# A fused attention and two-FFN kernel: whole token tiles through DRAM in FFN2, and another order of the seven block products of a pair

## The chip, the cores and the metric

The kernel runs on one core of a Trainium2 chip. The metric is the device time of one execution in microseconds, the median over the runs. A profile of one further execution comes with it; its span runs from the first to the last instruction of the program.

## The reference, cut to what matters

Sliding-window attention over 4 batches of 576 tokens with 8 heads gives x of 2304 tokens by 512. Two feed-forward layers follow; the change lies in the second.

```python
x = attention(q, k, v)                        # 2304 x 512, window of 64
h = np.maximum(x @ w_in, 0.0)                 # FFN1, 2048 wide
x = h * h @ w_out                             # 2304 x 512
h = x @ w2_in                                 # FFN2, 1024 wide
e = np.exp(h - np.max(h, axis=-1, keepdims=True))
solu = h * (e / (np.sum(e, axis=-1, keepdims=True) + 1e-09))
mu, var = np.mean(solu, -1, keepdims=True), np.var(solu, -1, keepdims=True)
out = ((solu - mu) / np.sqrt(var + 1e-06) * g_ln) @ w2_out
```

## The kernel before

Everything is fp32, computed on TensorE as three fp32r products per block: each operand is split into a high part (ScalarE copies it, which rounds) and a low part (VectorE subtracts the high part), and high*high, high*low and low*high are accumulated (`TERMS`).

**The planner.** No order is written out by hand. The kernel's Python first adds some 2,400 tasks with `add(engine, us, rank, fn, after, take, give, ...)`: a duration, a rank, the tasks that it waits for, and the buffers that it takes and gives back (`wb`, `wm`, `raw`, `g`, `a`, `b`, `t`, ...; `a`, `b` and `t` are PSUM tiles of the pools `ps_a`, `ps_b` and `ps_t`). `Plan.run` plays them through: of all tasks whose waits are met it takes the one that can start first, and the lower rank where two could start at once. Each engine gets its instructions in that order and runs them in order. `SHIFT` adds a number to the rank of single tasks, by their number. 51 filler matmuls (`warm`, line 1766, rank 900) stand wherever the planner sees nothing else for TensorE.

**The stages.** Attention and FFN1 are interleaved up to about 385 us. The sweep (line 1070, `swept`) finishes FFN1's last pass: it loads intermediates `r` from DRAM, splits them (`parted`, lines 1091 and 1094, tiles `g` and `gx`) and multiplies. The first weights of FFN2 are made meanwhile (`w2_operands`). FFN2 begins at 438.6 us and lasts to the end.

**FFN2.** `pair2` takes two token tiles of 128 at a time, nine pairs in all. The 256 x 1024 product of a pair with `w2_in` is made with seven block products in place of eight (a Strassen form): x is cut into A11, A12, A21, A22 (tile by half of the 512 inputs), the sums S1 to S4 are made from them on VectorE, and the weights have T1 to T4. A product is two times three matmuls of 512 columns (line 1543). The products add up in four PSUM banks named a, b, c, d:

```
P1 = A11 B11 (a)   P2 = A12 B21 (b)   P3 = S4 B22 (c)   P4 = A22 T4 (d)
P5 = S1 T1 (c)     P6 = S2 T2 (a)     P7 = S3 T3 (a)
C11 = P1 + P2      C12 = (P1 + P6) + (P5 + P3)
C21 = (P1 + P6 + P7) + P4             C22 = (P1 + P6 + P7) + P5
```

Where a bank is added to after it was needed as it stood, ScalarE copies it first (`keep1`, line 1549, tile `p`; `u2`, line 1553; `u3`, line 1557), and `total` (line 1568) makes each C block on VectorE from a bank and a copy or another term, with the running minimum that the softmax needs.

**Behind the products.** `behind` takes one tile of 128 tokens by 1024: exp on ScalarE (line 1625), the SoLU product on VectorE (1632), centring on ScalarE (1636), then a transpose. It is made of two VectorE transposes of 32 x 32 blocks (`blocks2`, line 1652, one per half of the 1024), a store to DRAM (`aside`, line 1656) and four loads with the blocks in their places (`across`, line 1664). ScalarE and VectorE split the loaded tile (`t_high`, line 1684; `t_low`, line 1688, tile `lnT`), and `mm_o` (line 1695) multiplies by `w2_out`, 12 matmuls for each half. All DMAs of this part are issued from SyncE's queue.

Of the kernel before, what the change touches and what calls it, by code (L numbers as in the profile page):

```python
# [20 lines left out]
P = 128  # L21
# [5 lines left out]
class Plan:  # L27
# [10 lines left out]
    SHIFT = {0: 19.99, 1: 13.18, 37: 14.79, 71: -15.08, 162: -7.47, 183: 14.39, 188: 6.06, 192: -2.38, 195: 10.82, 198: 10.82, 228: 5.72, 260: -3.03,  # L38
# [69 lines left out]
def kernel(  # L108
# [96 lines left out]
    with ExitStack() as c1:  # L205
# [1206 lines left out]
        def w2_operands(r, rank, homes):  # L1412
# [27 lines left out]
            for x in ("B11", "T2", "T3", "T1", "B21", "T4", "B22"):  # L1440
                if x in ("T1", "T4"):
                    when[x][1].append(ready["T2" if x == "T1" else "T3", r])
                ready[x, r] = split(hi[x], lo[x], *when[x], rank, 512, src[x], ["raw"] * (x in ("T1", "T4")))
                w2i[x, r] = hi[x], lo[x]
# [36 lines left out]
        ring = {}  # L1481
        kept = []
# [4 lines left out]
        def pair2(n, rank, rank_o):  # L1487
# [41 lines left out]
            def product(bank, x, w, begins, ends):  # L1529
                if begins and n < 2 and bank in "ad" and bank not in o:  # L1530
                    o[bank] = ps_a.tile([P, 512], F32, tag="a", name="ps_h2")
                elif begins and bank not in o:
                    if n in (0, 2):
                        kept.append(ps_b.tile([P, 2, 512], F32, tag="b", name="ps_h2"))
                    o.update(c=kept[0][:, 0], b=kept[0][:, 1])
                    if n > 1:
                        o.update(a=kept[1][:, 0], d=kept[1][:, 1])
# [59 lines left out]
            free = read_of.get(n - 1, {})  # L1597
            p1 = pe(0, "a", "A11", "B11", True, free.get("a", []) if n > 1 else [], take=["a"] if n < 2 else ["b"] * (n == 2))
# [15 lines left out]
            for m, k in enumerate((1, 0)):  # L1614
                behind(k, tiles[k][0], o, rank + LATE0 * (n == 0) + 0.1 * m, rank_o + m * 2 * mm(512), [f11, f12] if k == 0 else [f21, f22])
# [204 lines left out]
```

## Time and profile before

| | |
|---|---|
| median of 3 runs | 637.67 us (637.28 to 638.97) |
| the profiled execution | 637.17 us |
| its span | 635.4 us |
| mean granted TensorE clock | 0.999 |
| TensorE matmul busy | 623.2 us, 98% of the span |
| VectorE / ScalarE busy | 486.3 us (77%) / 431.0 us (68%) |

The profiled execution took 1.8 us more than its span and lies 0.5 us below the median. PE is TensorE's matmuls, PEld its weight loads, DVE is VectorE, ACT ScalarE, SP SyncE (SPq: its DMA issues). A matmul's record is longer than its turn, since the next one starts before it ends; stalls are therefore read from the distance between starts. Fillers count as busy.

### The profile page before, as it was taken

To read this page: it belongs to the slowest core of one execution; us is meant where nothing else is said; L and a number is where in the kernel's file an instruction comes from. 1 tells how busy PE (TensorE), PEld (TensorE's weight loads), DVE (VectorE), ACT (ScalarE), POOL (GpSimd) and SP (SyncE) were. 2 spreads that over 40 slices of the span, in tenths; PEclk is the share of its full clock that TensorE was granted. 3 is DMA by queue.
4 is the path that set the end of the run, shared out by engine and by line. 5 is a ranking of instruction groups with operands and counts; after the bars stand their busy time and mean duration, and the time that the engine had idled before them with its cause. 6 is when DMAs were issued, how large, how long until landed. Compare 5 with 4: busy or idle time off the path is not lost.

```text
span 635.4 us, 11735 instructions
## 1 busy us (share of the span) xinstructions
PE 623.2 (98%) x4009; PEld 523.6 (82%) x4009; DVE 486.3 (77%) x1129; ACT 431.0 (68%) x976; POOL 45.5 (7%) x80
## 2 busy tenths in 40 slices
PE   9999999999999999999999999999999999999997
PEld 4798888889889999998788887688778877778886
DVE  6999897497967653678899998998788927967450
ACT  5879776577877665657677766774677836866461
POOL 1000000001221110000000000000010200101000
PEclk9999999999999999999999999999999999999999
DMA  8888889447899999936776566864366642654451
GB/s 287 295 287 288 305 275 315 133 156 258 261 341 281 343 310 294 359 123 204 256 263 244 182 219 222 304 211 150 100 186 184 185 142 79 197 159 130 134 179 54
DMA packets 109260, 141.28 MB, mean 222 GB/s; under 512 B 9104, under 2 KB 75408, under 8 KB 109200
## 3 DMA queue, kind: packets, MB, share of 16 engines
q1 hardware_dynamic: 108512, 140.14, 66.8%
q8 instruction: 31, 0.51, 0.3%
q10 hardware_dynamic: 688, 0.39, 0.2%
q14 instruction: 29, 0.24, 0.1%
HBM read 90.69 MB, written 49.81 MB: 221 GB/s over the span
## 4 chain that ended last, share of the span: by engine, by line
PE 76%; DVE 9%; DMA 5%; ACT 3%; issue 3%; SPq 2%; POOL 0%; DVEq 0%; ACTq 0%; POOLq 0%
PE ps_h L936 18%; PE ps_h L1543 10%; PE ps_y L1256 10%; PE ps_o L1695 9%; PE ps_y L1070 8%; PE ps_y L707 7%; PE ps_h L691 6%; PE ps_s L436 2%; SPq L1664 2%; DMA tt_dram<-tt 2%; PE ps_warm L1766 2%; PE ps_v L519 2%; DVE e L1632 1%; DVE h L1568 1%; ACT e L451 1%
## 5 line engine op out<-in xcount | busy, mean ns | idle before, releaser
L1695 PE MATMUL ps_o<-w2o,lnT 128*128 128x512 f32 x432 | 100.4, 389 | 0.0
L1695 PEld LDWEIGHTS ps_o<-w2o,lnT 128*128 128x128 f32 x432 | 81.0, 188 | 17.2 <-issue 0.4
L1256 PE MATMUL ps_y<-g,wb 128*128 128x384 f32 x384 | 70.9, 335 | 0.0
L1256 PEld LDWEIGHTS ps_y<-g,wb 128*128 128x128 f32 x384 | 66.7, 188 | 0.5 <-issue 0.2
L1543 PE MATMUL ps_h<-w2i,xx 128*128 128x512 f32 x243 | 64.7, 393 | 1.8 <-DVE nmax L1568 1.0
L1070 PE MATMUL ps_y<-g,wb 128*128 128x512 f32 x234 | 58.3, 392 | 0.2 <-DVE g L1094 0.2
L1543 PEld LDWEIGHTS ps_h<-w2i,xx 128*128 128x128 f32 x243 | 45.2, 188 | 13.4 <-DVE nmax L1568 2.8
L936 PE MATMUL ps_h<-xa,wo 128*128 128x512 f32 (+1 forms) x192 | 53.0, 369 | 0.0
L1070 PEld LDWEIGHTS ps_y<-g,wb 128*128 128x128 f32 x234 | 43.6, 188 | 10.4 <-DVE g L1094 1.3
L936 PE MATMUL ps_h<-xb,wo 128*128 128x384 f32 (+1 forms) x192 | 51.2, 357 | 0.0
L707 PE MATMUL ps_y<-g,wb 128*128 128x512 f32 (+1 forms) x240 | 47.9, 352 | 0.0
L691 PE MATMUL ps_h<-x,wa 128*128 128x512 f32 (+1 forms) x240 | 47.4, 351 | 0.0
L936 PE MATMUL ps_h<-xo,wo 128*128 128x512 f32 (+1 forms) x128 | 47.2, 369 | 0.0
L451 ACT ACTIVATE e<-e,nmax 128x128 f32<-128x128 f32 x112 | 43.3, 390 | 2.2 <-DVE nmax L440 2.2
L707 PEld LDWEIGHTS ps_y<-g,wb 128*128 128x128 f32 x240 | 38.5, 189 | 6.3 <-issue 0.7
L691 PEld LDWEIGHTS ps_h<-x,wa 128*128 128x128 f32 x240 | 38.5, 189 | 6.1 <-issue 0.3
L936 PEld LDWEIGHTS ps_h<-xa,wo 128*128 128x128 f32 x192 | 35.2, 188 | 4.9 <-issue 0.3
L1543 PE MATMUL ps_h<-w2x,xx 128*128 128x512 f32 x135 | 37.2, 393 | 1.1 <-ACT p L1549 1.0
L936 PEld LDWEIGHTS ps_h<-xb,wo 128*128 128x128 f32 x192 | 34.6, 188 | 3.8 <-issue 0.5
L640 DVE TENSOR_TENSOR g<-r,g 128x384 fp32r<-128x384 f32 (+2 forms) x36 | 20.4, 569 | 21.6 <-ACT g L637 19.6
L1688 DVE TENSOR_TENSOR lnT<-l,lnT 128x512 fp32r<-128x512 f32 x36 | 24.5, 681 | 16.2 <-ACT lnT L1684 15.5
L1684 ACT ACTIVATE lnT<-l 128x512 fp32r<-128x512 f32 x36 | 22.4, 623 | 15.5 <-PE ps_o L1695 8.8
(181 smaller groups left out, 1258.6 us busy)
## 6 DMA issues: line engine op xcount, KB each, us to landing
wraw<-in_w_out SPq DMA_DIRECT2D x24, 511.8 KB, 5.0
wraw<-in_w_in SPq DMA_DIRECT2D x24, 511.8 KB, 5.5
t_dram<-h SPq DMA_DIRECT2D x36, 256.0 KB, 2.6
l<-t_dram SPq DMA_DIRECT2D x144, 64.0 KB, 2.0
vt<-in_v SPq DMA_DIRECT2D x32, 256.0 KB, 3.9
wo_dram<-wo SPq DMA_DIRECT2D x16, 512.0 KB, 4.5
wo<-wo_dram SPq DMA_DIRECT2D x16, 512.0 KB, 4.6
kt<-in_k SPq DMA_DIRECT2D x16, 384.0 KB, 5.2
```

What stands on the lines that cost most here:

```text
L436: T.matmul(to, qt[rows, i, hp, :], kt[rows, keys, hp, :], start=not begins, stop=not begins or hp == hps[-1])
L451: S.activation(out=o["er"][:, a, w], in_=s, func=AF.Exp, scale=SCALE if begins else -1.0, bias=o["nmax"][:, a, w : w + 1], accum_out=o["su ...
L640: V.tensor_tensor(out=o["g"][:, 1, :N], in0=o["r"], in1=o["g"][:, 0, :N].bitcast(F32), op=ALU.subtract)
L691: T.matmul(ps[:, :N], wa[kk][:, wi, c * P : c * P + P], xs[t][:, xi, c, n0:n1], start=n == 0, stop=n == 3 * DC - 1)
L707: T.matmul(acc[t, 0][d][:, n0:n1], wb[kk][:, wi, d * P : d * P + P], o["g"][:, xi, :N], start=kk == 0 and n == 0 and n0 == 0, stop=last an ...
L936: T.matmul(to[:, :N], w["t"][:, wi, off + c * P : off + c * P + P], (lo if xi else hi)()[:, c], start=begins and m == 0, stop=m == 5, skip ...
L1070: T.matmul(acc[name][d][:, :N], wb[kk][:, wi, col + d * P : col + d * P + P], q["g"][:, xi, :N], start=j == 0 and n == 0 and name not in ( ...
L1256: T.matmul(acc[t, half][d][:, :N], wb[kk][:, wi, d * P : d * P + P], q["g"][:, xi, :N], start=pos == 0 and n == 0, stop=pos == KF - 1 and ...
L1543: T.matmul(o[bank], o["xx", k][:, xi, at : at + P], w2i[w, r][wi][0](), start=begins and m == 0, stop=m == 5, skip_group_check=True)
L1684: S.activation(out=parts2(o["l", hf][:, 0]), in_=turned2(hf), func=AF.Copy)
L1688: V.tensor_tensor(out=parts2(l[:, 1]), in0=turned2(hf), in1=parts2(l[:, 0].bitcast(F32)), op=ALU.subtract)
L1695: T.matmul(o["o"], o["l", hf][:, xi, kk % 4, :], w2o[kk][:, wi, :], start=kk == 0 and n == 0, stop=kk == KF2 - 1 and n == 2)
```

## The change

Four things change, all but one in FFN2.

1. Token tiles go to DRAM and back whole: one store and four loads per tile, once both halves are transposed, in place of two stores and eight loads by halves. The last pair keeps its halves.
2. The products of a pair come in the order P1 P2 P5 P6 P4 P3 P7, before P1 P2 P6 P5 P7 P4 P3. P5 and P4 are copied out of their banks (`u5`, `u4`) where P1 + P6 + P7 was (`u3`); C22 and C21 are then summed from bank a and those copies. Banks a and d of odd pairs lie in `ps_t`, those of even pairs from the third on in `ps_b`; only the first pair takes them from `ps_a`. Tile 0 of a pair goes ahead of tile 1.
3. The weights of FFN2 are split in the order of the new products.
4. `SHIFT` has other numbers, for tasks of all stages; most lie in the sweep and after it.

```diff
-    SHIFT = {0: 19.99, 1: 13.18, 37: 14.79, 71: -15.08, 162: -7.47, 183: 14.39, 188: 6.06, 192: -2.38, 195: 10.82, 198: 10.82, 228: 5.72, 260: -3.03,
...
+    SHIFT = {0: 13.59, 3: 4.48, 4: -11.32, 22: -7.17, 37: 14.79, 71: -15.08, 162: -5.57, 188: 6.06, 192: -3.28, 195: 10.82, 198: 10.82, 202: -1.28,
...
+             1289: -1.64, 1297: -1.6, 1312: 1.85, 1317: 7.05, 1365: 7.1, 1457: 7.13, 1458: 6.02, 1459: 4.98, 1471: -17.49, 1493: -2.7, 1502: 16.22,
+             1504: 7.12, 1568: -7.42, 1572: -9.29, 1576: -9.35, 1580: -9.31, 1584: -9.27, 1585: 6.83, 1590: 3.97, 1592: -9.29, 1598: 10.55,
...
-            for x in ("B11", "T2", "T3", "T1", "B21", "T4", "B22"):
+            for x in ("B11", "B21", "T1", "T2", "T4", "B22", "T3"):
...
             def product(bank, x, w, begins, ends):
...
+                if begins and bank not in o:
+                    if n == 0 and bank in "ad":
+                        o[bank] = ps_a.tile([P, 512], F32, tag="a", name="ps_h2")
+                    elif n % 2 and bank in "ad":
+                        if (1, bank) not in banks:
+                            banks[1, bank] = ps_t.tile([P, 512], F32, tag="t", name="ps_h2")
+                        o[bank] = banks[1, bank]
+                    else:
+                        two = "cb" if bank in "cb" else "ad"
+                        if two not in banks:
+                            banks[two] = ps_b.tile([P, 2, 512], F32, tag="b", name="ps_h2")
+                        o[bank] = banks[two][:, two.index(bank)]
...
-            def u3():
-                o["u3"] = term("u3")
-                S.activation(out=o["u3"], in_=o["a"], func=AF.Copy)
+            def u4():
+                o["u4"] = term("u4")
+                S.activation(out=o["u4"], in_=o["d"], func=AF.Copy)
+
+            def u5():
+                o["u5"] = term("u5")
+                S.activation(out=o["u5"], in_=o["c"], func=AF.Copy)
...
-                total(1, 1, o["c"], o["u3"], True)
+                total(1, 1, o["a"], o["u5"], True)
...
-                total(1, 0, o["d"], o["u3"], False)
+                total(1, 0, o["a"], o["u4"], False)
...
-            p6 = pe(2, "a", "S2", "T2", False, [e1, p2])
+            f11 = add("DVE", 0.70, soon, c11, [p2, e1], take=["wb"])
+            p5 = pe(2, "c", "S1", "T1", True, [p2, *free.get("c", [])])
+            e5 = add("ACT", 0.60, soon, u5, [p5], take=["wm"])
+            p6 = pe(3, "a", "S2", "T2", False, [e1, p5])
             e2 = add("ACT", 0.60, soon, u2, [p6, *gone_by, *free.get("c", [])])
-            f11 = add("DVE", 0.70, soon, c11, [p2, e1], take=["wb"])
-            p5 = pe(3, "c", "S1", "T1", True, [p6, *free.get("c", [])])
-            p7 = pe(4, "a", "S3", "T3", False, [p5, e2])
-            e3 = add("ACT", 0.60, soon, u3, [p7], take=["wm"], give=["a"] * (n < 2))
-            p4 = pe(5, "d", "A22", "T4", True, [p7, *free.get("d", [])], take=["a"] * (n < 2))
-            f22 = add("DVE", 0.68, soon, c22, [p5, e3], take=["wb"])
-            f21 = add("DVE", 0.68, soon, c21, [p4, f22], give=["a", "wm"] if n < 2 else ["wm"])
-            p3 = pe(6, "c", "S4", "B22", False, [p4, f22], give=["wb"] * 4)
-            f12 = add("DVE", 0.68, soon, c12, [p3, f11, f21])
-            phase_of[n], read_of[n] = [p3], {"a": [e3], "b": [f11], "c": [f12], "d": [f21]}
+            p4 = pe(4, "d", "A22", "T4", True, [p6, *freer.get("d", [])], take=[own] if own else [])
+            e4 = add("ACT", 0.60, soon, u4, [p4], take=["wm"], give=["a"] * (n == 0))
+            p3 = pe(5, "c", "S4", "B22", False, [e5, p4])
+            f12 = add("DVE", 0.68, soon, c12, [p3, f11, e2])
+            p7 = pe(6, "a", "S3", "T3", False, [p3, e2], give=["wb"] * 4)
+            f22 = add("DVE", 0.68, soon, c22, [p7, e5], take=["wb"], give=["wm"])
+            f21 = add("DVE", 0.68, soon, c21, [p7, e4, f22], give=["wm"] + ["a"] * (n == 0))
+            phase_of[n], read_of[n] = [p7], {"a": [f22, f21], "b": [f11], "c": [f12], "d": [e4]}
...
-            for m, k in enumerate((1, 0)):
+            for m, k in enumerate((0, 1)):
...
-            by_pe = i in TURNED
+            by_pe, at_once = i in TURNED, not p["last"]
...
+            def part_c(x, hf):
+                return x if at_once else half_c(x, hf)
...
+                if at_once:
+                    p_ = [add("SP", 0.5, rank, lambda: aside(0), p_, late=2.2, give=["wb"])]
+                    p_ = [add("SP", 1.9, rank, lambda: across(0), p_, take=["g"], late=LATE_T + 0.4)] * 2
+                else:
+                    p_ = [add("SP", 0.5, rank, lambda hf=hf: aside(hf), [p_[hf]], late=1.9, give=["wb"] * hf) for hf in range(2)]
+                    p_ = [add("SP", 1.9, rank, lambda hf=hf: across(hf), [p_[hf]], take=["g"] * (1 - hf), late=LATE_T) for hf in range(2)]
```

## Rows read from the trace of the kernel before

**Rows 1.** The page's part 1: busy us, share of the span, instructions.
```profile
PE 623.2 (98%) x4009; PEld 523.6 (82%) x4009; DVE 486.3 (77%) x1129; ACT 431.0 (68%) x976; POOL 45.5 (7%) x80
```

**Rows 2.** Windows: length, busy us of each engine, clock, DMA share, GB/s.
```profile
385.00:438.60 53.60, 51.64 (x222) 40.64 (x221) 49.95 (x88) 37.26 (x69) 0.00 (x0) 1.00 0.68 224
517.00:537.00 20.00, 18.08 (x76) 14.12 (x77) 9.88 (x28) 8.88 (x15) 1.18 (x2) 1.00 0.25 75
```

**Rows 3.** PE's timeline in FFN2: start, length, matmuls; idle time and its releaser.
```profile
515.01 1.52 PE L1543 MATMUL ps_h<-w2i,xx 128*128 128x512 f32 x6
517.20 0.96 PE L1543 MATMUL ps_h<-w2x,xx 128*128 128x512 f32 x3 [0.67 <-ACT p L1549]
...
522.09 0.84 PE L1543 MATMUL ps_h<-w2i,xx 128*128 128x512 f32 x3
523.62 0.96 PE L1543 MATMUL ps_h<-w2i,xx 128*128 128x512 f32 x3 [0.69 <-ACT u L1557]
...
528.70 0.86 PE L1543 MATMUL ps_h<-w2i,xx 128*128 128x512 f32 x3
530.59 0.97 PE L1543 MATMUL ps_h<-w2i,xx 128*128 128x512 f32 x3 [1.03 <-DVE nmax L1568]
...
569.44 1.52 PE L1543 MATMUL ps_h<-w2i,xx 128*128 128x512 f32 x6
571.26 0.97 PE L1543 MATMUL ps_h<-w2x,xx 128*128 128x512 f32 x3 [0.30 <-ACT p L1549]
...
601.57 30.08 PE L1695 MATMUL ps_o<-w2o,lnT 128*128 128x512 f32 x132
```

**Rows 4.** PE's timeline ahead of the first output matmul.
```profile
456.69 1.69 PE L1766 MATMUL ps_warm<-ones 128*128 128x512 bf16 x4
458.02 1.75 PE L1543 MATMUL ps_h<-w2i,xx 128*128 128x512 f32 x6
459.61 2.33 PE L1766 MATMUL ps_warm<-ones 128*128 128x512 bf16 x10
461.88 2.97 PE L1695 MATMUL ps_o<-w2o,lnT 128*128 128x512 f32 x12
```

**Rows 5.** PE's waits from 385 to 636 us: in total, times, longest.
```profile
PE ps_y L1070 <- DVE gx L1094: 1.9, 2, 1.1
```

**Rows 6.** Groups by line, 440 to 640 us: busy, mean ns, idle before.
```profile
L1568 DVE CUSTOM_DVE_ANT_0 h<-ps_h,u,nmax 128x512 f32<-128x512 f32 x18 | 13.4, 744 | 2.0 <-PE ps_h L1543 1.0 <-DVE nmax L1568 0.5
L1557 ACT ACTIVATE u<-ps_h 128x512 f32<-128x512 f32 x9 | 5.4, 598 | 19.0 <-PE ps_h L1543 19.0
```

**Rows 7.** DMA issues: count, KB each, median us from issue to landing.
```profile
t_dram<-h SPq DMA_DIRECT2D x36, 256.0 KB, 2.6
l<-t_dram SPq DMA_DIRECT2D x144, 64.0 KB, 2.0
wo_dram<-wo SPq DMA_DIRECT2D x16, 512.0 KB, 4.5
x_dram<-y SPq DMA_DIRECT2D x1, 512.0 KB, 2.7
```

**Rows 8.** Timeline of the other engines around the first tile.
```profile
452.34 1.30 DVE L1652 STREAM_TRANSPOSE h<-e 128x512 f32<-128x512 f32 x2
453.07 1.24 SPq L1656 DMA_DIRECT2D t_dram<-h  x2
455.62 3.66 SPq L1664 DMA_DIRECT2D l<-t_dram  x8
459.38 0.61 ACT L1684 ACTIVATE lnT<-l 128x512 fp32r<-128x512 f32 x1
461.07 0.65 DVE L1688 TENSOR_TENSOR lnT<-l,lnT 128x512 fp32r<-128x512 f32 x1
462.91 0.69 DVE L1525 TENSOR_TENSOR xx<-xs,xx 128x512 fp32r<-128x512 f32 x1
```

**Rows 9.** Timeline of ACT near the end.
```profile
620.81 0.63 ACT L1684 ACTIVATE lnT<-l 128x512 fp32r<-128x512 f32 x1 [2.04 <-PE ps_o L1695]
```

More of the change, by code (lines that the diff above doesn't have):

```diff
@@ L1439, in w2_operands @@
                     "T2": ([t4], []), "T4": ([t4], [])}
-            for x in ("B11", "T2", "T3", "T1", "B21", "T4", "B22"):
-                if x in ("T1", "T4"):
-                    when[x][1].append(ready["T2" if x == "T1" else "T3", r])
-                ready[x, r] = split(hi[x], lo[x], *when[x], rank, 512, src[x], ["raw"] * (x in ("T1", "T4")))
+            for x in ("B11", "B21", "T1", "T2", "T4", "B22", "T3"):
+                if x in ("T2", "T3"):
+                    when[x][1].append(ready["T1" if x == "T2" else "T4", r])
+                ready[x, r] = split(hi[x], lo[x], *when[x], rank, 512, src[x], ["raw"] * (x in ("T2", "T3")))
                 w2i[x, r] = hi[x], lo[x]
@@ L1479, in term @@
             return raw_p.tile([P, 512], F32, tag="wm", name=name, bufs=WMB)
-        ring = {}
-        kept = []
+        ring, banks = {}, {}
         phase_of, read_of = {}, {}
@@ L1529, in product @@
             def product(bank, x, w, begins, ends):
[L1530 to L1537, printed above, removed]
+                if begins and bank not in o:
[10 more added lines that the diff above has]
+                        o[bank] = banks[two][:, two.index(bank)]
                 k, half = WHERE[x]
@@ L1596, in pair2 @@
             soon = rank - 41.25
-            free = read_of.get(n - 1, {})
-            p1 = pe(0, "a", "A11", "B11", True, free.get("a", []) if n > 1 else [], take=["a"] if n < 2 else ["b"] * (n == 2))
+            free, freer = read_of.get(n - 1, {}), read_of.get(n - 2, {}) if n > 2 else {}
+            own = {0: "a", 1: "t"}.get(n)
+            p1 = pe(0, "a", "A11", "B11", True, freer.get("a", []), take=[own] if own else ["b"] * (n == 2))
             e1 = add("ACT", 0.60, soon, keep1, [p1, *gone_by, *free.get("b", [])])
@@ L1655, in aside @@
             def aside(hf):
-                nc.sync.dma_start(out=half_c(t_dram[i].rearrange("p (b c j) -> p b c j", b=4, c=KF2), hf),
-                                  in_=half_c(o["h"].rearrange("p (b c j) -> p b c j", b=4, c=KF2), hf))
+                nc.sync.dma_start(out=part_c(t_dram[i].rearrange("p (b c j) -> p b c j", b=4, c=KF2), hf),
+                                  in_=part_c(o["h"].rearrange("p (b c j) -> p b c j", b=4, c=KF2), hf))
             def across(hf):
@@ L1663, in across @@
                 for b in range(4):
-                    nc.sync.dma_start(out=half_c(o["l4"][b * rows : b * rows + rows], hf),
-                                      in_=t_dram[i].rearrange("(a p) (b c j) -> b p a c j", a=4, b=4, c=KF2)[b][:, :, 4 * hf : 4 * hf + 4])
+                    nc.sync.dma_start(out=part_c(o["l4"][b * rows : b * rows + rows], hf),
+                                      in_=part_c(t_dram[i].rearrange("(a p) (b c j) -> b p a c j", a=4, b=4, c=KF2)[b], hf))
             def turned2(hf):
@@ L1728, in behind @@
                 r = add("ACT", 1.25, rank + 3, squares, p_)
-                p_ = [add("SP", 0.5, rank, lambda hf=hf: aside(hf), [p_[hf]], late=1.9, give=["wb"] * hf) for hf in range(2)]
-                p_ = [add("SP", 1.9, rank, lambda hf=hf: across(hf), [p_[hf]], take=["g"] * (1 - hf), late=LATE_T) for hf in range(2)]
+                if at_once:
[4 more added lines that the diff above has]
+                    p_ = [add("SP", 1.9, rank, lambda hf=hf: across(hf), [p_[hf]], take=["g"] * (1 - hf), late=LATE_T) for hf in range(2)]
                 r = add("POOL", 2.0, rank, root, [r], give=["wb"])
@@ L1739, in behind @@
                 l_free[k, hf] = [a]
-            if k == 0 and p["last"]:
+            if k == 1 and p["last"]:
                 b = add("ACT", 0.35, rank_o, lambda: scaled_half(0), [a, r], take=["r"])
```

14 rows, old and new, of the table SHIFT are left out of this document.

## The prediction

> **What bounds the kernel now.** I read the page's busy shares first: TensorE (PE) is busy in 623.2 of 635.4 us [rows 1]. So a change can win only where PE stands still, and an engine that gets faster beside it wins nothing by itself. Next came the windows by stage: the granted clock is 1.00 in both stretches shown, so time is lost to waits and not to the clock. In the sweep ahead of FFN2 (385 to 438.6 us) VectorE (DVE) is busy 49.95 of 53.6 us and PE misses 1.96; in the middle of FFN2 (517 to 537) PE misses 1.92 of 20 while DVE and ScalarE (ACT) are under half busy [rows 2]. The second stretch is short of neither engine: PE is held up by an order. The timeline of PE alone shows where.
>
> A product of six matmuls lasts 1.36 us: the run of 132 at the end starts one every (30.08 - 0.39) / 131 = 0.2266 us, 0.39 being the length of one record (the last start is 631.26) [rows 3]. With that rate the stalls can be read from start times. Six matmuls from 515.01 should end their turn at 516.37, the next starts at 517.20: 0.83 lost, waiting for `p`, the copy of P1. Three from 522.09, next at 523.62: 0.85, for `u`, a copy of the a bank. Three from 528.70, next at 530.59: 1.21, for the sum that must read bank c before P3 adds to it. Six from 569.44, next at 571.26: 0.46, for `p` again. Together 3.35 us [rows 3]. All four are one pattern: a bank is read out and added to again with a single product between.
>
> The other hole is the fill of FFN2 [rows 4]. Pair 1's last product starts at 458.02 after four filler matmuls from 456.69 (1.33 us), and ten more fillers from 459.61 stand ahead of the first output matmul (line 1695) at 461.88: 2.27 us. These fillers count as PE busy, so the busy share hides them.
>
> **The change part by part.**
>
> *Product order.* Before, P1 P2 P6 P5 P7 P4 P3: P6 adds to bank a once P1 is copied, with P2 as cover (1.36 us); P7 after the copy of P1+P6, with P5 as cover; P3 adds to c after a copy of a and a DVE sum in series (0.60 + 0.74 us, [rows 6], 1.34 and the hand-overs), with P4 as cover. After, P1 P2 P5 P6 P4 P3 P7: P6 has P2 and P5 ahead of it, P3 needs only the copy of P5 and has P6 and P4, P7 needs the copy of P1+P6 and has P4 and P3. Each cover becomes 2.72 us and no DVE sum stands in the chain any more. The longest stall above is 1.21 us and the added cover 1.36, so all four go: -3.35. The wait between pairs eases too: banks a and d alternate between two places, so the next P1 does not wait for sums of the pair before, and P5 meets bank c three products after P3 as before.
>
> Cost: one more copy per pair on ACT (P5 and P4 copied, P7 no longer), 9 x 0.60 = 5.4 us [rows 6]. ACT has 11.1 of 20 us free where the stalls are [rows 2]; PE's work hides it. If ACT has an exp or a square ahead of a copy, the copy is late by about one of those, and the doubled cover is what absorbs it. The sums on DVE stay four per pair. `c21` and `c22` now both follow the last product, so the second tile starts one sum (0.74 us) later; a tile waits much longer than that for its output matmuls, except in the fill, where the first tile counts. That one is now tile 0, ready after the sixth product as tile 1 was.
>
> *Whole tiles.* Per tile two stores and eight loads become one and four. Eight load issues take 3.66 us and two stores 1.24 [rows 8], so SyncE (SP) is spared 0.62 + 4 x 0.46 = 2.5 us a tile, for 16 of 18 tiles. What is queued behind them (loads of x, stores of the output) goes out earlier; no PE stall above ends in it, so I count nothing.
>
> It costs latency of the first half. Now its store goes out at 453.07, during the second DVE transpose (1.30 us for both); the loads start at 455.62, ACT splits at 459.38, DVE at 461.07, PE starts at 461.88 [rows 4, 8]. After, the store waits for the second transpose: +0.65. It is 512 instead of 256 KB: between +0.1 (2.7 against 2.6 us to landing) and +1.9 (4.5), the latter from stores in stages with heavier traffic; the loads, 128 instead of 64 KB, add between nothing and the same again [rows 7]. In the fill only one stream of tiles is moving, so I take the row of 2.7 for the store, another 0.1 for the loads: +0.85. At best it is 0, since ACT is done at 459.99 and DVE comes 1.08 later, being busy, which could absorb it all; at worst 0.65 + 1.9 + 1.9 = 4.45. PE has nothing else there before pair 2, whose last operand DVE starts at 462.91 and ends 0.69 later, at 463.60 [rows 8]; so unless that also moves, the fill's hole can grow by no more than 463.7 - 461.88 = 1.8. The stalls that the new order takes from pairs 0 and 1 return here as a longer wait for the same first tile: no gain. The second half arrives no later than now. Beyond the fill the loss lies behind a backlog of output matmuls; at the end ACT waits 2.04 us for PE to hand back a slot, not the other way [rows 9].
>
> The Trainium skill's page "DMA: Bandwidth & Descriptors", section "Anatomy of one DMA — SWDGE (gpsimd) path", puts a transfer at about 2.0 us plus its bytes at 436 GB/s. By that a 256 KB store takes an estimated 2.6 us, as the row has it, but a 512 KB one 3.2, and a 128 KB load 0.15 more than a 64 KB one; the fill would lose an estimated 1.4 us, and the change would win 1.95. The row of 2.7 us is a single transfer.
>
> *Rank shifts.* They change the planned order in all stages: tasks are numbered as they are added, and by that count most of the changed numbers (1568 to 1700) are loads of the sweep, moved by 9 to 12 us of rank against each other, and those just above are FFN2's first weights. PE's waits in the sweep are 1.9 us in two places, both for a split on DVE, a 93% busy engine [rows 2, 5]. Below, both could go: -1.9. Above, as many again could appear: +1.9. Nothing says which, so 0. The weights' order of splitting follows the products.
>
> **The sum.** -3.35 + 0.85 + 0 = -2.5 us. The profiled execution took 637.17 us, 1.8 beyond its span, and 0.5 less than the median of 637.67; 637.17 - 2.5 = 634.67, and 637.67 - 2.5 = 635.17 as a median; I say 635.1.
>
> **The rivals.**
>
> *More than forecast.* Fill and sweep close as well: pair 2's operands are prepared earlier, since ACT and DVE are not full there, and replace fillers (up to 1.33 + 2.27 = 3.6), or the two waits of the sweep go (1.9). Against it: the first tile's chain is no shorter. With 1.9 more and half of the fill: 637.67 - 3.35 - 1.9 - 1.8 + 0.85 = 631.5.
>
> *The stall only moves.* PE has many small waits for ACT and DVE, both in-order engines. If the new order on them puts a copy behind an exp and a square, or uses up the ready output matmuls in a burst, the two stalls for `p` stay (0.83 + 0.46) and the fill takes its 1.8: -3.35 + 1.29 + 1.8 = -0.26, or 637.4. For it: DVE is near full at the seam of sweep and FFN2. Against it: DVE and ACT are under half busy where the stalls are.
>
> *Slower: the sweep starves.* The new shifts start loads of the sweep earlier, and they take shared buffers and queue turns from the splits that feed PE. Two waits cost 1.9 now, 0.95 each [rows 5]. It decides the sign once it adds more than the 2.5 won, three further waits, and measurably at five: +4.75 - 2.5 = 2.2, or 639.9. For it: DVE's 93% in that stretch leaves no slack. Against it: those loads are moved to earlier, and late loads are what starve a split.
>
> **How the numbers follow.** Forecast (stalls gone, fill a little longer) 0.42: 633.7 to 636.2. More than forecast 0.22: 630.5 to 633.7. Stall only moves 0.21: 636.2 to 638.8. Slower 0.15: 638.8 to 642. A measurement of this kernel tells 0.3% (1.9 us) from no change: faster means under 635.8, slower over 639.6. Of the forecast's 0.42 about 0.35 lies under 635.8; with 0.22 faster is 0.57. Of the slower rival's 0.15 about 0.12 lies beyond 639.6, and the rest, 0.31, is the same. The predicted time is 635.1; from 631.0 to 638.8 leaves out some 0.04 below and 0.15 above. The forecast's own range is 633.7 to 636.2.
>
> **What would show it.** In the profile after, PE should have no wait for `p`, `u` or a sum between the products of a pair; products of one pair should stand in runs with 0.227 us between starts. The hole ahead of the first output matmul, now 1.33 + 2.27 us of fillers [rows 4], should lie in one piece behind pair 1 and be longer by 0.85, at most 1.8. Stores to `t_dram` should number 20 (16 + 4) instead of 36, loads from it 80 instead of 144, and land in 2.7 and 2.1 us. If the store takes over 4 us, or output matmuls come in a long burst and PE then waits, the fill or the backlog was mis-sized; if PE's waits in the sweep pass 4 us, the shifts were.

## The result and the profile after

| | before | after |
|---|---|---|
| median | 638.32 us (637.28 to 639.49) | 631.17 us (630.62 to 631.53) |
| runs | 4 | 4 |
| ratio, with its 95% interval | | 0.9887 [0.9865, 0.9908] |
| the profiled execution | 637.17 us | 631.49 us |
| its span | 635.4 us | 629.7 us |

The change wins 7.15 us between the medians and 637.17 - 631.49 = 5.68 us between the two profiled executions; the forecast was 2.5. Before scatters more than after: over 19 runs beside the later experiments its median was 637.86 (636.25 to 641.27). What follows is worked out between the profiles, and the 1.5 us between 5.68 and 7.15 is that scatter: the profiled run of before lies 1.15 under its median of 638.32, that of after 0.32 over its own.

The first two parts of the page after, busy time and the windows, answer to [rows 1, 2].

```profile
PE 621.6 (99%) x4009; PEld 523.7 (83%) x4009; DVE 484.6 (77%) x1129; ACT 434.8 (69%) x985; POOL 45.3 (7%) x80
```

```profile
385.00:438.60 53.60, 52.16 (x225) 41.07 (x224) 51.53 (x91) 37.47 (x69) 0.00 (x0) 1.00 0.68 225
517.00:537.00 20.00, 20.00 (x90) 16.57 (x89) 14.39 (x35) 13.69 (x23) 1.75 (x4) 1.00 0.47 159
```

PE does the same 4009 matmuls, all 51 fillers among them, and is busy 1.6 us less. The fillers have moved: 8 stand inside FFN2, where 14 stood, and four behind its last output matmul. From 517 to 537 it has no gap at all, where it missed 1.92 of 20 us; the granted clock is 1.00 in both stretches, as before. PE's list of waits from 380 us on has four lines, as before, but they add up to 2.1 us in place of 4.6:

```profile
PE ps_y L1070 <- DVE y L1157: 1.0, 1, 1.0
PE ps_h L1546 <- ACT u L1560: 0.7, 1, 0.7
PE ps_h L1546 <- ACT u L1556: 0.2, 1, 0.2
PE ps_y L1070 <- DVE gx L1094: 0.2, 1, 0.2
```

PE's timeline shows what stands where the fill of FFN2 was [rows 4] (L1546 is a product, L1707 an output matmul, L1782 a filler, L1070 the sweep):

```profile
446.16 1.52 PE L1070 MATMUL ps_y<-gx,wb 128*128 128x512 f32 x6
447.52 2.12 PE L1782 MATMUL ps_warm<-ones 128*128 128x512 bf16 x7
449.29 1.04 PE L1546 MATMUL ps_h<-w2i,xx 128*128 128x512 f32 x3
...
459.04 0.39 PE L1782 MATMUL ps_warm<-ones 128*128 128x512 bf16 x1
459.08 1.04 PE L1546 MATMUL ps_h<-w2i,xx 128*128 128x512 f32 x3
...
468.33 0.96 PE L1546 MATMUL ps_h<-w2x,xx 128*128 128x512 f32 x3 [0.70 <-ACT u L1560]
...
469.82 11.04 PE L1707 MATMUL ps_o<-w2o,lnT 128*128 128x512 f32 x48
...
489.22 0.98 PE L1546 MATMUL ps_h<-w2x,xx 128*128 128x512 f32 x3 [0.19 <-ACT u L1556]
...
490.73 11.07 PE L1707 MATMUL ps_o<-w2o,lnT 128*128 128x512 f32 x48
```

Pair 0 starts before the sweep's last twelve matmuls, pair 1 follows at 449.29, and then the whole of pair 2, from 459.08 on, stands where ten fillers were. The first output matmul starts at 469.82 instead of 461.88: the first tile is 8 us later, and PE has work all the same. From there whole pairs (42 products' matmuls) and two whole tiles (48 output matmuls) take turns. The other engines' timeline says why pair 2 is ready:

```profile
458.12 0.70 DVE L1664 STREAM_TRANSPOSE h<-e 128x512 f32<-128x512 f32 x1
458.74 0.65 DVE L1524 TENSOR_TENSOR xx<-xs,xx 128x512 fp32r<-128x512 f32 x1
458.85 0.32 SPq L1668 DMA_DIRECT2D t_dram<-h  x1
...
461.97 1.83 SPq L1676 DMA_DIRECT2D l<-t_dram  x4
...
468.17 1.15 ACT L1696 ACTIVATE lnT<-l 128x512 fp32r<-128x512 f32 x2
```

DVE ends pair 2's last operand (line 1524) at 459.39, where before it ended at 463.60 [rows 8], and the first tile's transposes (line 1664), its store and its loads stand between and behind these splits. On the page the tile's transfers are half as many, twice as large, and land in 2.9 us each [rows 7]:

```profile
t_dram<-h SPq DMA_DIRECT2D x16, 512.0 KB, 2.9
l<-t_dram SPq DMA_DIRECT2D x64, 128.0 KB, 2.9
```

**Where the 5.7 us came from**, by starts in the two traces. FFN2's length below runs from its first product to the end of its last output matmul, less 12 x 0.2267 = 2.72 us where twelve matmuls of the sweep lie inside; "sweep's end" is the start of the first product plus these 2.72.

| | before | after | |
|---|---|---|---|
| sweep's end | 438.61 | 435.28 + 2.72 = 438.00 | -0.6 |
| fillers inside FFN2 | 14 in 3.60 us | 8 in 1.81 us | -1.8 |
| PE's gaps inside FFN2, those of 0.07 us and more beyond a 0.2267 us turn | 5.39 | 2.11 | -3.3 |
| FFN2's length | 193.05 | 187.92 | -5.1 |

### The profile page after: what moved, and what is told of

It reads as the page before. It is cut to its first block, busy times and chain, and to the rows that moved or that the text cites. A ratio compares the mean times of both kernels' runs of the same rounds, so it can differ in the third digit from the quotient of the medians.

```text
span 629.7 us, 11572 instructions
## 1 busy us (share of the span) xinstructions
PE 621.6 (99%) x4009; PEld 523.7 (83%) x4009; DVE 484.6 (77%) x1129; ACT 434.8 (69%) x985; POOL 45.3 (7%) x80
## 4 chain that ended last, share of the span: by engine, by line
PE 86%; DVE 5%; DMA 4%; ACT 3%; issue 1%; SPq 1%; POOL 0%; ACTq 0%; DVEq 0%; POOLq 0%
PE ps_h L936 22%; PE ps_o L1707 14%; PE ps_y L1070 10%; PE ps_h L1546 10%; PE ps_y L1256 10%; PE ps_y L707 7%; PE ps_h L691 6%; PE ps_s L436 3%; PE ps_v L519 2%; PE ps_warm L1782 1%; DMA l<-t_dram 1%; DMA kt<-in_k 1%; DMA r_dram<-u 1%; DMA t_dram<-h 1%; PE ps_v L522 1%
## 5 line engine op out<-in xcount | busy, mean ns | idle before, releaser
L1707 PE MATMUL ps_o<-w2o,lnT 128*128 128x512 f32 x432 | 99.1, 389 | 0.0
L1707 PEld LDWEIGHTS ps_o<-w2o,lnT 128*128 128x128 f32 x432 | 81.1, 188 | 16.9
L1546 PE MATMUL ps_h<-w2i,xx 128*128 128x512 f32 x243 | 62.8, 391 | 0.0
L1070 PE MATMUL ps_y<-g,wb 128*128 128x512 f32 x234 | 58.3, 391 | 1.1 <-DVE y L1157 1.0
L1546 PEld LDWEIGHTS ps_h<-w2i,xx 128*128 128x128 f32 x243 | 45.6, 188 | 9.6
L1070 PEld LDWEIGHTS ps_y<-g,wb 128*128 128x128 f32 x234 | 43.7, 188 | 11.4 <-DVE y L1157 1.4
L1546 PE MATMUL ps_h<-w2x,xx 128*128 128x512 f32 x135 | 37.0, 393 | 0.9 <-ACT u L1560 0.7
L461 POOL TENSOR_TENSOR e<-e,sums 128x512 f32<-128x512 f32 x16 | 18.5, 1179 | 205.0 <-PE ps_h L936 141.9
```

Source lines behind the costliest of these rows:

```text
L461: eng.tensor_tensor(out=o["er"][:, a], in0=o["er"][:, a], in1=o["sums"][:, a].unsqueeze(2).to_broadcast([P, HP, W]), op=ALU.mult)
L1070: T.matmul(acc[name][d][:, :N], wb[kk][:, wi, col + d * P : col + d * P + P], q["g"][:, xi, :N], start=j == 0 and n == 0 and name not in ( ...
L1546: T.matmul(o[bank], o["xx", k][:, xi, at : at + P], w2i[w, r][wi][0](), start=begins and m == 0, stop=m == 5, skip_group_check=True)
L1707: T.matmul(o["o"], o["l", hf][:, xi, kk % 4, :], w2o[kk][:, wi, :], start=kk == 0 and n == 0, stop=kk == KF2 - 1 and n == 2)
```

## The experiments

Two theories stood at the start. **The products:** the covers of 2.72 us take the stalls away, as forecast, and the shifts in FFN2 close the fill. **The queues:** the rank shifts put instructions into an order on the in-order engines in which no product's copy stands behind a wait for a load, and pair 2 ahead of the first tile; the product order itself matters little. (A third, that the spared DMA issues closed the fill, fell with e1.) Parts were undone in the kernel after or put alone into the kernel before; the new early shifts, those ahead of FFN2, were not run without the new weights' order. Tasks kept their shift's number where a part adds or drops tasks. Lengths are read as in the table above, each from one profile; profiled runs lie up to 1.3 us from the median of their kernel (e2, e10, e13), so some tenths decide nothing.

| kernel | median (range), us | ratio to before | sweep's end | FFN2 | fillers |
|---|---|---|---|---|---|
| after, tiles in halves (e1) | 630.52 (630.22 to 631.55) | 0.9884 [0.9842, 0.9926] | 437.40 | 187.58 | 8 |
| after, no FFN2 shifts (e2) | 635.61 (634.36 to 638.26) | 0.9961 [0.9943, 0.9980] | 437.10 | 191.75 | 12 |
| after, old products (e3) | 631.52 (631.12 to 632.14) | 0.9897 [0.9862, 0.9932] | 437.28 | 188.50 | 12 |
| before, new products and weights' order (e4) | 643.12 (642.22 to 644.33) | 1.0080 [1.0059, 1.0102] | 445.61 | 191.09 | 12 |
| after, old products, banks, halves (e5) | 633.07 (632.66 to 633.51) | 0.9931 [0.9915, 0.9946] | 437.30 | 190.34 | 12 |
| after, three of seven FFN2 shifts (e6) | 631.64 (631.11 to 632.25) | 0.9908 [0.9891, 0.9926] | 437.34 | 188.28 | 11 |
| after, old early shifts (e7) | 639.78 (638.08 to 641.34) | 1.0025 [1.0008, 1.0042] | 446.02 | 188.67 | 12 |
| before, no FFN2 shifts (e8) | 637.23 (636.05 to 638.42) | 0.9988 [0.9972, 1.0005] | 439.06 | 192.71 | 14 |
| before, weights' order alone (e9) | 649.07 (648.22 to 650.73) | 1.0162 [1.0129, 1.0195] | 446.46 | 196.25 | 14 |
| before, new products, old weights' order (e10) | 636.01 (634.66 to 638.67) | 0.9968 [0.9948, 0.9988] | 438.20 | 190.97 | 14 |
| after, old banks (e11) | 634.01 (633.79 to 634.83) | 0.9926 [0.9897, 0.9954] | 438.15 | 190.88 | 12 |
| before, whole tiles alone (e12) | 639.00 (636.56 to 640.34) | 1.0009 [0.9987, 1.0031] | 440.66 | 192.63 | 14 |
| after, both early edits undone (e13) | 633.98 (632.69 to 635.50) | 0.9938 [0.9915, 0.9961] | 438.61 | 188.57 | 14 |

**e1, the kernel after with its tiles in halves again.**

```diff
-            by_pe, at_once = i in TURNED, not p["last"]
+            by_pe, at_once = i in TURNED, False
```

> The changed kernel with the tiles in halves again (two stores and eight loads a tile); every task of the planner keeps its shift. Theory A (the product order took the stalls inside the pairs, the shifts in FFN2 closed the fill, whole tiles are worth nothing): 630.7 to 632.0 us. Theory B (the spared DMA issues brought pair 2's operands and the tiles earlier, and that closed the fill): 633 us or more, with pair 2's first product at least 1.8 us later.

630.52 us, just under the first range: whole tiles are worth nothing in the kernel after, -0.3 us of FFN2 if anything. The first tile is not what PE waits for there.

**e2, the kernel after without its seven shifts in FFN2.**

```diff
-             1786: 11.48, 1787: 10.78, 1804: 21.08, 1840: 37.96, 1846: 11.51, 1864: 10.81, 1900: 4.34}
+             }
```

> The changed kernel without its seven rank shifts for tasks of FFN2 (numbers 1786 to 1900). Theory A: pair 2's operands come behind the first tile's transposes again, the fill's hole returns, 634 to 637 us; no stalls inside the pairs. Theory B: the shifts do not matter, within 1 us of 631.2.

635.61 us, 4.4 over the kernel after, and FFN2 is 3.8 longer. PE's timeline, with the stall of pair 2 (two smaller ones of 0.8 and 0.3 us follow) and the first output matmuls:

```profile
459.02 1.04 PE L1538 MATMUL ps_h<-w2i,xx 128*128 128x512 f32 x3
...
462.64 0.84 PE L1538 MATMUL ps_h<-w2x,xx 128*128 128x512 f32 x3
466.37 0.96 PE L1538 MATMUL ps_h<-w2x,xx 128*128 128x512 f32 x3 [2.89 <-ACT p L1544]
...
473.28 11.04 PE L1699 MATMUL ps_o<-w2o,lnT 128*128 128x512 f32 x48
```

Neither theory had this: pair 2 still stands ahead of the first tile, and stalls inside. ACT's timeline in the same stretch:

```profile
463.65 1.15 ACT L1688 ACTIVATE lnT<-l 128x512 fp32r<-128x512 f32 x2 [2.03 <-DMA l<-t_dram]
464.71 1.13 ACT L1637 ACTIVATE e<-e,sums 128x1024 f32<-128x1024 f32 x1
465.75 0.57 ACT L1544 ACTIVATE p<-ps_h 128x512 f32<-128x512 f32 x1
```

The copy `p` of P1 could be made from about 460.8: P1's six matmuls start at 459.02, and the next product at 460.59 (in e6, where pair 2 starts at 459.04, it is made at 460.86). It is made at 465.75, because ACT stands 2.03 us before it at the split of the first tile, whose load has not landed, and then centres a tile. New products, a cover of 2.72 us, and yet a stall of 3 us: a cover hides lateness only up to its own length, and this copy comes 4.9 us late, behind a wait for a load. The kernel before had the same picture at the stall of 517.20 [rows 3], in its ACT timeline:

```profile
514.20 0.63 ACT L1684 ACTIVATE lnT<-l 128x512 fp32r<-128x512 f32 x1 [2.31 <-DMA l<-t_dram]
...
516.03 0.63 ACT L1684 ACTIVATE lnT<-l 128x512 fp32r<-128x512 f32 x1 [0.62 <-DMA l<-t_dram]
516.57 0.58 ACT L1549 ACTIVATE p<-ps_h 128x512 f32<-128x512 f32 x1
```

There P1 began at 513.65, behind a burst of 84 output matmuls from 494.61 on. ACT came to the next tile's split before its load had landed, and the copy stood behind two such waits, 0.62 us of the second after P1 was done. ACT is under half busy in the stretch [rows 2]; it was not short of time but stood in its order. The Trainium skill's page "PSUM — Partial Sum Buffer", section "Engine vs sequencer instructions", says that ScalarE's, VectorE's and GpSimdE's queues are "strict FIFO"; both timelines agree, with 2.03 and 0.62 us of idle ACT ahead of a copy that could have run.

**e3, the kernel after with the old product order** (P1 P2 P6 P5 P7 P4 P3, P7 copied and not P5 and P4; the tiles of a pair in the old order; whole tiles, banks, weights' order and shifts of after).

```diff
-            p5 = pe(2, "c", "S1", "T1", True, [p2, *free.get("c", [])])
-            e5 = add("ACT", 0.60, soon, u5, [p5], take=["wm"])
-            p6 = pe(3, "a", "S2", "T2", False, [e1, p5])
+            p6 = pe(2, "a", "S2", "T2", False, [e1, p2])
...
+            p3 = pe(6, "c", "S4", "B22", False, [p4, f22], give=["wb"] * 4, number=False)
```

> The changed kernel with the products in the old order P1 P2 P6 P5 P7 P4 P3 and the copy u3 in place of u4 and u5; whole tiles, banks, weights' order and shifts stay. Theory A: the stalls inside the pairs return, 634 to 637 us, of it 3.3 us from waits for p, u and the sum. Theory C (the order itself is worth little, the shifts did it all): under 632.5.

631.52 us. The products theory would have had it lose about 3 us; FFN2 is 0.58 longer. One stall is left, the sum that reads bank c, and it stands in the fill:

```profile
469.03 1.65 PE L1548 MATMUL ps_h<-w2i,xx 128*128 128x512 f32 x6 [1.42 <-DVE nmax L1573]
470.52 11.04 PE L1705 MATMUL ps_o<-w2o,lnT 128*128 128x512 f32 x48
...
489.56 2.88 PE L1705 MATMUL ps_o<-w2o,lnT 128*128 128x512 f32 x12
```

From there on one output half (12 matmuls) stands ahead of the last product of each pair, which is all the cover that the sum needs. With the new queues the old product order stalls nowhere else.

**e4, the kernel before with the new product order** (with its banks, the order of the two tiles and the weights' splitting order; old shifts, halves).

> The kernel before with the new product order, its banks and the order of weights and tiles alone; halves and the old shifts stay. Theory A: under 1 us of stalls inside the pairs, but the old shifts leave pair 2 late, so the fill costs 4 to 7 us where it cost 3.6: 635 to 640. If the order alone were the gain, as the first term of the prediction has it: 635.0.

643.12 us, slower than before. FFN2 is 1.96 shorter, but the sweep ends 7.0 later. PE's timeline there:

```profile
416.03 2.88 PE L1072 MATMUL ps_y<-g,wb 128*128 128x512 f32 x12
421.84 2.93 PE L1072 MATMUL ps_y<-g,wb 128*128 128x512 f32 x6 [2.93 <-ACT ys L1176]
424.56 5.70 PE L1072 MATMUL ps_y<-gx,wb 128*128 128x512 f32 x24
```

and its windows before and behind that wait:

```profile
418.50:421.80 3.30, 0.41 (x2) 0.00 (x0) 3.30 (x7) 3.04 (x7) 0.00 (x0) 0.92 0.93 302
421.80:426.50 4.70, 4.66 (x15) 3.73 (x16) 4.67 (x9) 3.01 (x6) 0.00 (x0) 0.70 0.53 173
```

PE waits 2.93 us for ACT to empty a bank, while DVE and ACT are both all but fully busy. Then it pays a second time: six matmuls take 424.56 - 421.84 = 2.72 us, 0.453 each on average where 0.2267 is a turn at full speed, and the granted clock of the stretch is 0.70: 0.50, the half level (1.2 GHz), from 421.80 to 424.60, and at or near the full one (2.4 GHz) behind that. Whether the weights' order or the products caused it was left to e9 and e10.

**e5, the kernel after with old products, old banks and halves**, and with the tiles in the old order, so that of the change only the shifts and the weights' order are left.

> The changed kernel with the old product order, the tiles in halves and the old places of banks a and d: of the change only the rank shifts, the order of the weights' splitting and nothing else are left. Theory S (the gain is the order on the queues that the shifts make: pair 2 in the fill, outputs between the pairs): 631 to 633.5 us. Theory K (the second place of banks a and d lets pairs 1 and 2 run ahead): the fill's hole returns, 634.5 or more.

633.07 us: 4.7 of the 637.73 measured beside it are gone without one new product, copy, bank or whole tile; FFN2 is 2.7 shorter than before.

**e6, the kernel after with three of its seven FFN2 shifts:** 1786 (the centring of pair 0's first tile, 11.48 later), 1787 (its first transpose, 10.78) and 1804 (the first transpose of the second tile, 21.08).

```diff
-             1786: 11.48, 1787: 10.78, 1804: 21.08, 1840: 37.96, 1846: 11.51, 1864: 10.81, 1900: 4.34}
+             1786: 11.48, 1787: 10.78, 1804: 21.08}
```

> The changed kernel with three of its seven shifts in FFN2, those that put the centring and the first transposes of pair 0's two tiles back (numbers 1786, 1787, 1804). Theory S: pair 2's operands come ahead of these transposes and the fill is closed by that alone, 631 to 632.5 us. If the other four shifts do it: 634 to 636, as without any.

631.64 us and FFN2 at 188.28: these three carry 3.5 of the 3.8 us that e2 lost. They do nothing but make the first two tiles wait. Pair 2 starts no earlier than in e2:

```profile
459.04 1.05 PE L1538 MATMUL ps_h<-w2i,xx 128*128 128x512 f32 x3
```

What goes is the stall inside it. DVE starts the first tile's transposes at 456.24 and not at 449.75, and ACT comes to that tile's split at 466.80 and not, waiting, at 463.65; by then the copy of P1 has long been made.

**e7, the kernel after with the old shifts ahead of FFN2** (all numbers below 1769 as before).

> The changed kernel with the old shifts for every task ahead of FFN2 and the new ones in it. Prediction's term for the earlier stages (0, between -1.9 and +1.9): 631.2, at most 633.1. Theory S extended (the early shifts also let pair 0 start ahead of the sweep's last products): over 633.5, with a hole in the fill.

639.78 us. FFN2 keeps nearly all of its gain (188.67), but the sweep ends at 446.02, 8 us late, with the same wait as in e4 and matmuls at 0.33 us behind it. So the early shifts are worth 8 us once the weights' order has been changed; with that put back as well (e13) the sweep ends at 438.61.

**e8, the kernel before without its six FFN2 shifts.**

> The kernel before without its six shifts in FFN2. Theory S: the stalls of 2.9 us between 515 and 531 came from a burst of seven output halves that these shifts made; without them outputs stand by threes behind each pair, those stalls go and the time is 634 to 636.5. If the old product order is the cause of the stalls, as the prediction has it: they stay, 637 to 639.

637.23 us, no change that can be told. The burst of 84 output matmuls is gone, and with it the three stalls of 515 to 531 us, as the first theory expected; but two new ones of 0.57 us, at the first output matmuls, and 1.26 us, in pair 3, came, and the time did not follow: the gaps shrink only from 5.39 to 4.21 us, and the fillers take 0.54 us more. So the six old shifts are worth nothing that can be told; it is not shifts in FFN2 as such that pay, but the three of e6.

**e9, the kernel before with the weights' splitting order alone.**

```diff
-            for x in ("B11", "T2", "T3", "T1", "B21", "T4", "B22"):
-                if x in ("T1", "T4"):
+            for x in ("B11", "B21", "T1", "T2", "T4", "B22", "T3"):
+                if x in ("T2", "T3"):
```

> The kernel before, with only the splitting order of FFN2's weights changed to B11 B21 T1 T2 T4 B22 T3; products, banks, shifts and halves as before. Theory 1: the 7 us that the sweep lost when the new product order was put alone into the kernel before come from this splitting order, whose loads the old shifts had spaced for another one. Then FFN2's first product starts 5 to 8 us later than 438.61 here too, with a PE wait of about 3 us for ACT's ys ahead of it and matmuls at half the clock behind it, and the median is 642 to 647 (pair 0 also meets T2 and T3 later than its products want them). Theory 2: the loss came from the copies of the new product order, which ACT must make in the middle of the sweep. Then FFN2 starts within 1.5 us of 438.61, no such wait stands in the sweep, and the median is 637 to 640.

649.07 us, more than either bound: the sweep's end slips by 7.85 and FFN2 loses 3.2. The wait is that of e4, at the same place, with no new copy in the kernel, so e4's loss came from the weights' order:

```profile
423.03 2.93 PE L1070 MATMUL ps_y<-g,wb 128*128 128x512 f32 x6 [2.95 <-ACT ys L1174]
425.76 4.54 PE L1070 MATMUL ps_y<-gx,wb 128*128 128x512 f32 x18
```

In ACT's queue the copy that PE waits for stands behind a split of the sweep that waits 2.05 us for DVE, and behind four splits of weights:

```profile
418.76 0.63 ACT L1091 ACTIVATE g<-r 128x512 fp32r<-128x512 f32 x1 [2.05 <-DVE gx L1094]
419.30 0.61 ACT L343 ACTIVATE w2i<-ws 128x512 fp32r<-128x512 f32 x1
419.82 1.90 ACT L343 ACTIVATE w2x<-ws 128x512 fp32r<-128x512 f32 x3
...
422.38 0.60 ACT L1174 ACTIVATE ys<-ps_y 128x512 f32<-128x512 f32 x1
```

**e10, e4 with the old weights' order**, so the new products, banks and tile order alone, under the old queues.

> The kernel before with the new product order, its copies, its banks and the order of the two tiles, but the old splitting order of the weights; old shifts, halves. Theory 1 (the splitting order made the loss): FFN2's first product stays within 1.5 us of 438.61, the stalls inside pairs are gone, the fill keeps some 14 fillers or grows by one stall, FFN2 lasts 190.5 to 192 us against 193.04, and the median is 635.5 to 637.5. Theory 2 (the copies made it): FFN2 starts 5 us late or more, and the median is about 643 as before with both.

636.01 us, ratio 0.9968 [0.9948, 0.9988]. The sweep ends where it did (438.20) and FFN2 is 2.08 shorter. The forecast had sized this part at 3.35. Behind a burst of 96 output matmuls from 493.26 on, pairs 4 and 5 lose 0.12 us; the kernel before lost 3.47 in them behind its burst of 84, the first three stalls of [rows 3] among it, so there the longer cover does what the forecast said. Two stalls inside pairs are left, 0.94 and 0.50 us, both for the copy of P4; the 14 fillers stay, in one piece, with the wait that the forecast saw behind them:

```profile
457.24 3.20 PE L1777 MATMUL ps_warm<-ones 128*128 128x512 bf16 x14
460.65 0.50 PE L1706 MATMUL ps_o<-w2o,lnT 128*128 128x512 f32 x1 [0.21 <-ACT lnT L1695]
461.97 5.91 PE L1706 MATMUL ps_o<-w2o,lnT 128*128 128x512 f32 x23 [0.82 <-DVE lnT L1699]
```

**e11, the kernel after with one place for banks a and d.**

```diff
-            p1 = pe(0, "a", "A11", "B11", True, freer.get("a", []), take=[own] if own else ["b"] * (n == 2))
+            p1 = pe(0, "a", "A11", "B11", True, free.get("a", []) if n > 1 else [], take=["a"] if n < 2 else ["b"] * (n == 2))
```

> The changed kernel with one place for banks a and d instead of two: pair 1 takes the two single banks of pair 0, and all later pairs the same double bank. Theory 1: the second place lets pair 1's first product start before pair 0's sums are read, and its loss shows in the fill alone: FFN2 lasts 1.0 to 2.0 us longer than 187.9, median 632.3 to 633.3. Rival: the queues' order hides it as it hides the product order; FFN2 within 0.5 us of 187.9, median 630.8 to 631.9.

634.01 us; FFN2 is 2.96 longer, more than expected. Most of it lies in the fill: 12 fillers from 457.20 to 461.34 ahead of pair 2, 4.14 us against the 1.81 of the kernel after. But eight of the twelve start 0.43 us apart and only the rest 0.22, though the granted clock of the stretch is 1.00; at 0.22 the twelve would have ended 8 x 0.21 = 1.7 us sooner. DVE ends pair 2's last operand at 460.61 here, 1.2 us later than in the kernel after. So by estimate the second place is worth 1.2 to 3 us of FFN2 (2.96, with or without those 1.7); what slows the fillers is open.

**e12, the kernel before with whole tiles alone.**

> The kernel before with whole tiles alone (one store of 512 KB and four loads of 128 KB for 16 of the 18 tiles), old product order, banks and shifts. The prediction's term: the first output matmul starts 0.85 us later than 461.88 (0 to 1.8), and the median is 638.3 to 639.5. Rival: whole tiles are worth nothing here either, as they were worth nothing when the changed kernel was put back to halves: first output matmul within 0.3 us of 461.88 and the median 637 to 638.

639.00 us, no change that can be told, 1.0009 [0.9987, 1.0031]. In the fill PE's timeline shows

```profile
463.97 0.47 PE L1700 MATMUL ps_o<-w2o,lnT 128*128 128x512 f32 x1
465.14 2.80 PE L1700 MATMUL ps_o<-w2o,lnT 128*128 128x512 f32 x11 [0.70 <-DVE lnT L1693]
```

The first output matmul comes 463.97 - 440.66 = 23.31 us after the first product, 23.27 before; the second waits 465.14 - 463.97 - 0.23 = 0.95 us more. That is the +0.85 of the forecast, one matmul late. The rest of FFN2 gives 1.4 back, and its sweep ended 2.05 later, for which the change gives no reason that I can show; sweeps differ by that much between profiles (below).

**e13, the kernel after with both early edits undone** (old shifts ahead of FFN2 and old weights' order).

> The changed kernel with the shifts ahead of FFN2 and the weights' splitting order both put back as before; products, banks, whole tiles and the seven FFN2 shifts as changed. Theory 1 (the gain is the products' and banks' 2.1 us and the FFN2 shifts' work in the fill, the early edits are worth nothing as a pair): sweep ends within 0.8 us of 438.0, FFN2 lasts about 188, median 631 to 632. Theory 2 (the early edits are needed, since they let pair 0 start behind the last but twelve matmuls of the sweep, so that ACT and DVE get through pair 1 and pair 2's operands in time): a whole pair 0 and pair 1 without a gap, then about 14 fillers in one piece as with the products alone, FFN2 190 to 191.5, median 633.5 to 635.5.

633.98 us, in the second theory's range; the profiled run, 632.69, is the fastest of its ten and lies between the two. By this profile FFN2 lasts 188.57 and the sweep ends at 438.61, as the first theory had it; its picture is the second theory's:

```profile
457.65 3.20 PE L1774 MATMUL ps_warm<-ones 128*128 128x512 bf16 x14
460.50 1.05 PE L1538 MATMUL ps_h<-w2i,xx 128*128 128x512 f32 x3
...
470.11 0.96 PE L1538 MATMUL ps_h<-w2x,xx 128*128 128x512 f32 x3 [0.83 <-ACT u L1552]
...
471.61 8.55 PE L1699 MATMUL ps_o<-w2o,lnT 128*128 128x512 f32 x37
```

Pairs 0 and 1 run through, 14 fillers wait for pair 2, and pair 2 stands ahead of the first tile with the old early shifts too. So the early edits as a pair are worth 0.6 us of sweep and 0.65 of FFN2 between profiles, and 2.8 between medians.

**The sum in two orders.** By FFN2's length, from before to after:

| first the products | us | first the queues | us |
|---|---|---|---|
| new products, banks, tile order (e10) | -2.08 | all shifts, weights' order (e5) | -2.71 |
| FFN2 shifts and whole tiles (e13) | -2.40 | banks and whole tiles (e3) | -1.84 |
| early shifts and weights' order (after) | -0.65 | product order, copies, tile order (after) | -0.58 |

Both come to -5.13, and the sweep adds -0.6. A row of 0.6 lies within what single profiles can tell. The parts do not add up one by one: the product order is part of a gain of 2.1 under the old queues and worth 0.6 under the new ones, because both it and the shifts take the same stalls away. The -0.6 of the sweep is from one pair of profiles. In the seven with the new early edits the sweep ended at 437.10 to 438.15, in the five with both old ones at 438.20 to 440.66, and the middle values, 437.34 and 438.61, are 1.3 us apart; that may be part of what the medians show beyond the profiles.

## Why the forecast was right in direction and wrong in size

- **In-pair stalls, -3.35:** the sum of gaps agrees, -3.3, but in part by luck. The four stalls went; two others came, 0.86 us in pair 2 and 0.35 in pair 3; and smaller gaps that the forecast had not counted fell from 2.04 to 0.90. The reason given was half of it. The stalls were put down to a cover of one product; e2 has the cover of two and stalls 3 us, e3 has the cover of one and stalls once. Under the old queues the longer cover hides most of ACT's lateness (e10: FFN2 2.08 shorter); how late ACT's copy is depends on what stands ahead of it, above all a split that waits for a load.
- **No wait for `u` left:** wrong. P7 was counted with P4 and P3 as cover. In pair 2 the copy of P1+P6 ended at 466.97 and P7 started at 468.33, right behind the copy of P4 (467.69 to 468.28, behind two splits that took 0.93 us). In pair 3 P7 waited for the copy of P1+P6 alone. In pair 2 banks a and d are halves of one double tile, in pair 3 they are two tiles; that this link makes P7 wait for P4's copy is argued from the code, not tried. It costs 0.86 us in the kernel after, 0.94 in e10, 0.99 in e13.
- **The fill, +0.85:** this is the step that failed. It read "PE has nothing else there before pair 2 [...]; so unless that also moves, the fill's hole can grow by no more than [...] 1.8". That did move. The latency itself was right (0.95 in e12), but with pair 2 ahead of the first tile nothing waits for it: -1.8 measured, 2.6 us from the forecast. The order of the queues moved pair 2. With the new products and all the old shifts it stood behind the first tile (e10: 467.72 against 460.65); with the new FFN2 shifts and whole tiles added, ahead of it (e13: 460.50 against 471.61), and whole tiles alone do not move it (e12). The early edits without any FFN2 shift have it ahead as well (e2).
- **Whole tiles:** worth nothing in the kernel after (e1), and nothing that can be told in the kernel before (e12), where the loss at the first tile came as forecast and 1.4 us came back elsewhere in FFN2, for a reason not traced. Landing was put at 2.7 and 2.1 us; both rows say 2.9. The estimate worked out from the Trainium skill's page "DMA: Bandwidth & Descriptors", section "Anatomy of one DMA — SWDGE (gpsimd) path", was 3.2 us for the store, above the row, and by the same fit it would be 2.3 for a load, below the row; the fit is for DMAs issued on another path than SyncE's, and the estimated fill loss of 1.4 did not come.
- **Second place for a and d:** counted at nothing beyond an easier start of the next pair; some 1.2 to 3 us of FFN2 in the kernel after (e11).
- **Rank shifts, "Nothing says which, so 0":** the cause of the failed step. The forecast looked for their effect in the sweep, where the net is -0.6. But it had the list of the FFN2 shifts: 1786, 1787 and 1804 hold back the centring and transposes of pair 0, and its own row showed DVE ending pair 2's operands behind the first tile [rows 8]. Numbering the tasks of FFN2 would have pointed to it. Which of the early edits puts pair 2 ahead in e2 is not shown. The rival "more than forecast" named this, with 631.5 us, and was given 0.22; its "against" (the first tile's chain is no shorter) is true and does not matter.
- **The sweep starves:** it didn't, but the new weights' order without the new early shifts costs 8 us of sweep, in both kernels (e7, e9), against the rival's 4.75; with both, or with neither, the loss is not there. The rival had put it down to the new shifts; whether these starve the sweep under the old weights' order was not run.

The account closes: forecast -3.35 + 0.85 + 0; measured -3.3 - 1.8 - 0.6 = -5.7.

## What to carry to other kernels

When a planner writes the queues of in-order engines, a rank is an edit of the program: number the tasks that it moves and follow each past its neighbours on ACT, DVE and SP before it is costed at nothing. More work between two products hides a late copy only up to its own length, so look first at what stands ahead of the copy in its queue, above all an instruction that waits for a load. Put first into the queue what feeds the bound engine with a long piece of work, here a whole pair ahead of the first tile, and let the latency run behind it. And do not change the order of the data alone under queues tuned for another: here that cost 8 us (e7, e9).

## What was not expected of the hardware

- A wait of PE can cost more than its length. Behind the 3 us in e4 and e9 six matmuls took 0.453 and (425.76 - 423.03) / 6 = 0.455 us each on average, the first one included, against the 0.2267 of a full-speed turn; the granted clock of the windows behind the wait is 0.70 and 0.67, with 0.50, the half level, in the first 2.8 us of each. In the profiled run of e2 PE stood as long (its starts are 463.10 and 466.37; in e4 418.52 and 421.84), and there the clock stayed at 1.00 and the next six matmuls took 0.22 to 0.34 each. The nine other runs of e2 have a mean granted clock of 0.995 to 0.997, like those of e4, and took 1.0 to 3.9 us longer, so there it may have fallen too. What tells the two apart no run here shows. The Trainium skill's page "TensorE: Matmul & The Clock Gate", section "What's actually happening", has two levels of the clock, set by how busy PE has been; that the matmuls took about twice as long agrees.
- At the full clock the first matmul behind a wait takes 0.34 us instead of 0.2267, and the first behind a filler 0.42 (by starts in e2, at 466.37 and 459.02): 0.1 to 0.2 us a stall on top of the wait that the profile names.
- Eight fillers in a row took 0.43 us each in e11 at a granted clock of 1.00, twice their usual 0.22; the first three of the four fillers at 456.69 in the kernel before did so too, which is why four of them fill 1.33 us [rows 4]. That was not followed up.
